# Duo attention into a gated FFT convolution: one hand-ordered list of 988 operations, in a new sequence and with 115 of them on another engine

## The chip, the core and the metric

The kernel runs on one core of a Trainium2 chip. The core's engines work side by side, each through its own list of instructions: TensorE (PE) for matmuls, VectorE (DVE), ScalarE (ACT) and GpSimd (POOL) for everything elementwise, and SyncE (SP), which here only issues DMA transfers. The metric is device microseconds for one execution. Three runs of the kernel before took 185.37, 185.87 and 186.39 us, so its time is the median, 185.87 us.

## The reference

Inputs are q, k and v of shape (4 batches, 8 heads, 768 positions, 64), a weight `w_proj` (512 x 1536), a filter (768 x 512) and a weight `w_out` (512 x 512), all float32. Four heads attend causally to everything ("retrieval", kind R), the other four only to 4 sink positions and a window of 64 (kind L). The attention's output is then gated and convolved along the sequence:

```python
scores = scale * np.matmul(q, k.transpose(0, 1, 3, 2))
scores = np.where(mask, scores, -1e9)            # causal, or sinks and window
a = np.exp(scores - scores.max(-1)); a = a / (a.sum(-1) + 1e-9)
x = np.matmul(a, v)                              # then heads side by side: (4, 768, 512)
x1, x2, x3 = np.split(x @ w_proj, 3, axis=-1)
y = x1 * np.fft.irfft(np.fft.rfft(x2, axis=1) * np.fft.rfft(filter_fft, axis=0), axis=1) * x3
return y @ w_out
```

(The quoted code is shortened; `is_retrieval` is the per-head vector that chooses the mask, and the reference's shapes are as told above.)

## The kernel before

**Units of work.** Attention goes by head pairs `n` = 0 to 15: batch `n // 4`, and within it the pairs in an order that gives the kinds RR, LL, RL, LL (6, 3, 5 and 3 chunks of scores). The convolution goes by batch. Its Fourier transforms are matmuls with tables `G` and `Gi` built at the start; the transform is split into folds so that it takes fewer products.

**The names.** Every step of the program is an operation with a short name, and each operation is one or a few instructions. For a pair n:

- `lk`, `lq`, `lv`: loads from DRAM on SP's queue (L876, L898). Pairs 0 and 1 have their q and k loaded before the list begins.
- `ck`, `cq` (or `cqk` for n of 8 and more), `cv`: casts to bf16 (through the helper `ev`, L533 to L541). `vx`, `vs`, `ks`: small copies of the rows for windows and sinks; `kz` sets their buffers to zero beforehand.
- `T`: transposes of q and k. For n below 8 on PE (L923), with `E` as eviction from PSUM; for n of 8 and more by DMA on SP's queue (L933).
- `sc`: score matmuls (L961), which use 64 rows of PE; `sb`: matmuls that add the mask for n below 4 (L972); `ex`: exponential on ACT (L978); `mk`: masks by multiplication on DVE for n of 4 and more (L988 to L1008).
- `at`: probabilities times v, with a column of ones that gives the sums (L1021); `rec` and `nm`: reciprocal and quotient on DVE (L1027, L1038).
- `tn`, `te`: transposes of the result and their eviction (L1094; some by DMA at L1103), which make `xT`, the left side of the projections.
- `fd`, `fe`, `fA`, `fS`, `fb`, `fr`: sums and differences of the folds (mostly through the helper `two`, L543); `W` (L1074 to L1082) and its eviction `We`.

For a batch b: `X` (L1125), spectrum of x2, and its eviction `Xe`; `pa`, `pb`, `pc`: products with the filter's spectrum, with `sw` as swaps of halves by DMA (L1150); `c`: inverse transform (L1190); `ce` its eviction; `x1` and `x3`: projections (L1160), `xs` eviction of one; `cv` with a batch, third and half (`cv0.1.0`): product of the convolution with the projection (L1201); `g` and `y`: gating products (L1179, L1183, L544); `o`: output projection (L1220, L1225); `oe`: eviction; `st`: store (L1243 to L1265). For the filter: `lfilt` (L739, issued on POOL's queue), `fold0`, `fold1` (L760, L756), `F` (L768), `H` (L775, L777). `lw` and `lwo` load the weights, also on POOL's queue (L747, L752). `chk` and `gd0` to `gd4` work out on DVE and PE whether the head flags and the sums allow this fixed program, and the program closes with the reading of a word (L1277).

**What sets the order.** A string `FAST` holds the names in one sequence, written out. The program walks through it once, and every instruction goes to its engine's list in that order:

```python
for word in FAST.split():
    name, _, slot = word.partition("@")
    name, _, eng = name.partition("/")
    now.update(slot=slot, engine=eng)
    ops[name]()
```

`@0` to `@3` names one of four PSUM slots of two banks each, which an operation may use when the last reader of the tile before it in that slot is done. `/v`, `/p`, `/s` and `/d` place a word on DVE, POOL, ACT or SP's DMA queue; words without a letter have a fixed engine. Each engine works strictly in its order: an instruction that waits holds up all that stand behind it on that engine. The same holds for the two queues that issue transfers, SP's and POOL's. Data dependences and slot reuse are turned into semaphores by the framework.

Of the kernel before, what the change touches and what calls it, by code (L numbers as in the profile page):

```python
# [1361 lines left out]
```

## Time and profile before

| | |
|---|---|
| median of 3 runs | 185.87 us (185.37 to 186.39) |
| profiled execution, span | 186.0 us |
| mean granted PE clock | 0.993 of full |
| PE busy | 171.6 us, 92% |
| DVE busy | 152.5 us, 82% |
| ACT busy | 142.2 us, 76% |
| POOL busy | 83.5 us, 45% |
| moved by DMA | 33.44 MB, 180 GB/s on average |
| chain that ended last | PE 65%, DMA 16%, ACT 4%, DVE 4% |

A line `L961 PE MATMUL f_sc<-f_qkT 64*128 64x128 bf16 x252 | 13.7, 218 | 0.7 <-DMA ...` reads: line 961 of the kernel, engine, operation, tile written and tile read, shape, how many; then their busy time in us and the mean ns of one; then how long the engine sat idle just before them and what ended that. In the table by stage each row is a stretch of the execution, followed by its length, then the busy time of each engine with its count of instructions, the granted clock, the busy share of DMA and the rate. In the list of waits a row is the waiting instruction, what released it, the total in us, how often, and the longest. In the chain that ended last a row is a start time, a length and what ran. Times are in us from the first instruction.

### The profile page before, as it was taken

The page shows a single profiled execution, that of the slowest core. Times are in us where ns is not written, and L with a number is a line of the kernel's source. Part 1 is how long each engine was busy: PE and PEld are TensorE (multiplying, and loading weights), DVE is VectorE, ACT ScalarE, POOL GpSimd, SP SyncE. Part 2 cuts the span into 40 slices and gives each one's busy share as a digit, 9 for nine tenths or more (in the row PEclk, how much of TensorE's full clock was granted, in tenths as well). Part 3 has the DMA queues.
Part 4 walks back from the last instruction along what each step waited for, and adds up shares of the span by engine and source line. Part 5 has one row for each costly group of instructions (what it writes and reads, how often), then busy time and mean ns, then how long its engine had stood idle before and what let it go on. Part 6 is the DMA issues. An engine that isn't in the chain of part 4 may idle for free.

```text
span 186.0 us, 4370 instructions
## 1 busy us (share of the span) xinstructions
PE 171.6 (92%) x1685; PEld 102.2 (55%) x1702; DVE 152.5 (82%) x297; ACT 142.2 (76%) x186; POOL 83.5 (45%) x99
## 2 busy tenths in 40 slices
...
GB/s 163 305 305 194 257 272 244 260 215 130 211 224 217 104 217 222 177 149 221 216 239 201 223 203 171 127 252 222 124 102 40 118 0 131 40 4 113 188 281 108
DMA packets 76836, 33.44 MB, mean 180 GB/s; under 512 B 66058, under 2 KB 73226, under 8 KB 76810
## 3 DMA queue, kind: packets, MB, share of 16 engines
...
q10 hardware_dynamic: 146, 0.13, 0.2%
q14 instruction: 12, 0.10, 0.1%
HBM read 24.64 MB, written 6.29 MB: 166 GB/s over the span
## 4 chain that ended last, share of the span: by engine, by line
PE 65%; DMA 16%; ACT 4%; DVE 4%; SPq 3%; POOL 3%; issue 2%; POOLq 0%
PE f_x_ps L1160 20%; PE f_out_ps L1225 10%; PE f_X_ps L1125 10%; DMA f_filt<-in_moe_filter_fft_dram 7%; PE f_c_ps L1190 7%; PE f_sc L961 6%; PE f_att L1021 4%; DMA f_qkT<-f_qk_bf 4%; DMA f_v_f<-in_v_dram 3%; SPq L898 3%; DMA qk_ahead<-in_q_dram 2%; PE f_xt_ps L1094 2%; PE f_F_ps L768 1%; POOL f_fo L544 1%; PE f_W_ps L1082 1%
## 5 line engine op out<-in xcount | busy, mean ns | idle before, releaser
L978 ACT ACTIVATE f_pT<-f_sc 128x1024 bf16<-128x1024 f32 (+2 forms) x68 | 58.3, 914 | 4.1 <-PE f_sc L972 2.1
L1160 PE MATMUL f_x_ps<-f_xT,f_wproj 128*128 128x384 bf16 x256 | 48.4, 326 | 0.1
L1160 PEld LDWEIGHTS <-f_wproj 128*128 128x128 bf16 x256 | 23.5, 98 | 15.6 <-issue 0.4
L961 PE MATMUL f_sc<-f_qkT 64*128 64x128 bf16 (+3 forms) x328 | 21.1, 242 | 2.2 <-ACT f_pT L978 0.8
L1125 PE MATMUL f_X_ps<-f_wproj,f_xh 128*128 128x512 bf16 x91 | 22.1, 379 | 0.3
L1225 PE MATMUL f_out_ps<-f_wout,f_gy 128*128 128x512 bf16 x85 | 22.0, 379 | 0.3
L544 POOL TENSOR_TENSOR f_gy<-turns,f_gy 128x768 bf16<-128x768 bf16 x7 | 11.6, 1669 | 20.8 <-DVE f_gy L1179 11.3
L1190 PE MATMUL f_c_ps<-f_Gi,f_P 128*128 128x384 bf16 x96 | 18.7, 326 | 0.1
L1021 PEld LDWEIGHTS <-f_pT 128*128 128x128 bf16 x472 | 16.4, 97 | 4.0 <-issue 1.5
L541 ACT COPY f_o<-f_out_ps 128x1024 f32<-128x1024 f32 (+2 forms) x15 | 11.5, 788 | 8.8 <-PE f_out_ps L1225 8.8
L961 PEld LDWEIGHTS <-f_qkT 64*128 64x128 bf16 x328 | 11.1, 94 | 12.6 <-issue 8.4
L1201 DVE TENSOR_TENSOR turns<-angle,f_c_ps 128x384 bf16<-128x384 f32 x32 | 16.4, 547 | 1.7 <-ACT angle L541 1.3
L1021 PE MATMUL f_att<-f_v_aug,f_pT 128*128 128x65 bf16 x392 | 17.3, 193 | 0.4 <-DVE f_attn L1038 0.4
L544 POOL TENSOR_TENSOR f_fo<-f_attn 128x384 bf16<-128x384 bf16 x11 | 10.9, 1003 | 14.6 <-PE f_W_ps L1082 12.2
L1038 DVE TENSOR_TENSOR f_attn<-f_att,f_recs 128x768 bf16<-128x768 f32 x16 | 15.3, 954 | 0.4
L541 ACT CAST f_X<-f_X_ps 128x1024 bf16<-128x1024 f32 x11 | 11.1, 1016 | 5.9 <-PE f_X_ps L1125 5.9
L544 POOL TENSOR_TENSOR f_br<-f_fo,f_uv 128x256 bf16<-128x256 bf16 x9 | 6.9, 766 | 18.7 <-DVE f_uv L544 9.1
L1125 PEld LDWEIGHTS <-f_xh 128*128 128x128 bf16 x96 | 8.9, 98 | 10.5 <-issue 1.0
L537 POOL CAST f_qk_bf<-qk_ahead 128x768 bf16<-128x768 f32 (+1 forms) x10 | 11.4, 1149 | 4.4 <-DMA qk_ahead<-in_k_dram 4.3
L1225 PEld LDWEIGHTS <-f_gy 128*128 128x128 bf16 x92 | 8.5, 98 | 8.8 <-issue 0.4
L541 ACT CAST f_xh<-f_W_ps 128x768 bf16<-128x768 f32 x12 | 9.5, 801 | 4.6 <-PE f_W_ps L1078 4.6
L1190 PEld LDWEIGHTS <-f_P 128*128 128x128 bf16 x96 | 9.1, 98 | 6.0
...
## 6 DMA issues: line engine op xcount, KB each, us to landing
...
```

The costliest lines, as they stand in the source:

```text
L537: nc.gpsimd.tensor_copy(out=out, in_=in_)
L541: nc.scalar.copy(out=out, in_=in_)
L544: (nc.gpsimd if now["engine"] == "p" else nc.vector).tensor_tensor(out, a, b, op)
L961: nc.tensor.matmul(sc[:, bank, col:col + 128 * cnt], lhsT=keys, rhs=qkT(n)[rows, 0, 128 * i:128 * (i + cnt)], start=(col == 0 or not biase ...
L978: nc.scalar.activation(out=pT(n)[:, c, :, 0:w], in_=held[f"sc.{n}.{c}"][:, :, 0:w], func=AF.Exp, scale=SCALE)
L1021: nc.tensor.matmul(att[:, hh, 65 * i:65 * i + 65], lhsT=pT(n)[:, c, bank, col:col + 128], rhs=values, start=(z == 0), stop=(z == len(here) ...
L1038: nc.vector.tensor_mul(attn(n).rearrange("p i hh d -> p hh i d"), rows[:, :, :, 0:64], recs()[:, n][:, :, :, None].to_broadcast([128, 2, N ...
L1125: nc.tensor.matmul(ps[:, u, :], lhsT=xh(b)[:, cc, chain, 128 * part:128 * part + 128], rhs=wproj()[:, cc, DM:2 * DM], start=(cc == 0), sto ...
L1160: nc.tensor.matmul(ps[:, s, 0:HS], lhsT=wproj()[:, cc, part * DM + cb * 128:part * DM + (cb + 1) * 128], rhs=xT(b)[:, cc, s * HS:s * HS + HS],
L1190: nc.tensor.matmul(ps[:, r, 0:HS], lhsT=P(b)[:, t, u, ch], rhs=Gi()[:, tile_no], start=(m == 0), stop=(m == 2))
L1201: fn(conv[:, half * HS:half * HS + HS], held[f"evs.{b}.{cb}"], held[f"c_ps.{b}.{cb}"][:, 1, 0:HS])
L1225: nc.tensor.matmul(ps[:, i % 2, :], lhsT=gy(b)[:, cb, i * 128:(i + 1) * 128], rhs=wout()[:, cb, :], start=(cb == 0), stop=(cb == NC - 1))
```

## The change

Only the string `FAST` changes. The set of 988 names is the same, and no operation's content or shape differs. What differs:

- the sequence of the words, and with it each engine's order, the order of the loads on SP's queue and of those on POOL's queue, and the PSUM slots;
- the engine of 115 casts, copies, sums and products: DVE to POOL 32, POOL to DVE 29, DVE to ACT 22, ACT to DVE 21, ACT to POOL 8, POOL to ACT 3.

The sequence was drawn up with a picture of the loads in which those under way at the same time share the DMA engines packet by packet.

The diff, cut to its beginning (up to the filter's `H` steps and the first `X`), the stretch from `W4` to the products of pair 6, the stretches around `T15` and `fb10`, and its end:

```diff
--- before.py
+++ after.py
@@ -61,66 +61,65 @@
 FAST = """
-angle2 angle1 turns1 turns2 wrap0 ones1 wrap2 blank2@0 ck0/p T0.1@2 wrap1 cq0/s blank0@1 ck1/p sin1 T0.0 size
-blank1@3 lk3 E0.0/v E0.1/v cos2 mtab3 T1.1@0 sin2 sc0.4@3 cos1 sc0.2@1 btab sb0.2 sc0.0@2 sb0.0 lq2 cq1/v cq2/p ex0.2
-T1.0 alt lq3 ex0.0 sc0.1@1 sb0.1 sb0.4 Gt0@2 E1.0/v E1.1/v sc0.3@0 ex0.4 sb0.3 ex0.1 sc1.1@3 lk2 Ge0/v sb1.1 sc0.5@2
-ex0.3 sc1.0@1 kz0/v cq3/p ex1.1 sb0.5 lv0 lv1 ck3/v ks1/p ck2/v lv2 cv0/p T2.0@0 sb1.0 ones0 ones2 T2.1 ex0.5 sc1.2@2
-T3.1@3 ex1.0 E2.0/v E2.1/v E3.1/s sb1.2 at0.1@1 ex1.2 at0.0 rec0 kz1/v T3.0 sc2.0@0 sc2.4@2 Gh0 nm0/v E3.0/s cv1/p
-kz2/p lv3 lfilt lk5 vx1/v sb2.0 ex2.4 sc3.1@3 Gt1@2 cv3/p ex2.0 vs1/v at1.1@1 lq5 Ge1/s sb3.1 sc2.1@0 ks2/p Gk1 sb2.1
-ex3.1 at1.0 ex2.1 tn0@2 cv2/s ck5/p Gh1 rec1 lk4 sc2.3@3 Gk0 sc3.0@0 te0/v sc2.2@2 lq4 nm1/v lk6 sb2.2 sb3.0 ex2.3
-fd0/v T5.1@1 fe0/v W0.0@3 lw1.0 vx3/v cq5/p vs2/v ck4/p vx2/v W0.1 ks3/v ex2.2 E5.1/s vs3/v ex3.0 at2.0@2 T5.0 We0/v
-E5.0/s at2.1 sc3.2@3 tn1@0 rec2 nm2/v lk7 te1/v sb3.2 tn2@1 fd1/v ex3.2 sc5.1@2 cq4/s te2/v fold1 lq6 fold0 T4.1@0
-at3.1@3 ex5.1 lv4 at3.0 fe2/v T4.0 F2.1@1 E4.0/s lw1.1 F2.0 fe1/v F0.1@2 fd2/v F0.0 rec3 E4.1/s nm3/v mk5.1 H0.0/v
-W1.0@0 H2.1/s W1.1 H2.0/s H2.2/s W2.1@3 W2.0 fd3/p H0.1/v sc5.0@1 We1/s sc4.2@0 ck6/p ex5.0 lw0.0 H0.2/v W3.0@2 ks5/p
-fe3/v We2/v cq6/p ex4.2 W3.1 We3/v sc4.0@1 sc4.1@3 ex4.0 ex4.1 F1.0@0 F1.1 sc4.3@2 sc4.4@1 X0.2.1@3 ck7/p H1.1/v
...
-lk10 cv0.1.0 cv0.1.1 vs6/s W5.0@1 vx6/s W5.1 at6.0@3 ce0.0/s vx7/s at6.1 y0.1/p g0.2 c0.3.1@2 c0.3.0 We5/s cv0.0.1
-ce0.3/s cv0.0.0 sc8.4@0 sc8.1@1 rec6 ex8.4 nm6/v lq10 lv8 ex8.1 W4.0@3 cqk9/p y0.0/v W4.1 We4/s c0.2.1@0 c0.2.0
...
-fA10/v W9.0@0 x12.0.0@3 ex12.1 ce1.1/s W9.1 fr10 vx13/s cv1.1.0 x12.0.1 mk12.0 c1.0.0@2 We9/s fb10/p cv12/p c1.0.1
-cv1.1.1 fA11/p xs2.0/v c1.3.1@0 W10.0@1 W10.1 fS11/p ce1.0/s fb11/p fr11 x32.0.1@3 x32.0.0 c1.3.0 We10/s vs13/s
...
-T15 at12.0@1 sc14.1@2 sc13.2@0 ex13.2 at12.1 rec12 X2.2.1 pb2.1/p nm12/v x12.2.1@0 x12.2.0 ex14.1 tn12 pb2.0/v
-sc14.4@2 sc14.0@1 Xe2.2/s xs2.2/s mk13.2 fe12/v ex14.4 fd12/v st0.3 o1.1.0@3 mk13.1 sc15.0@0 sc15.1@2 pc2.0/v ex14.0
...
-y3.3/v o2.3.1 o2.2.1 gd3@3 gd4 x33.3.0@0 x33.3.1 g3.3 o3.0.0@2 o3.1.0@3 o3.1.1 oe2.3/s oe3.1/s o3.0.1 o3.5.0@1 st2.3
-oe3.5/s o3.2.0@0 oe3.0/s o3.2.1 o3.3.0@3 oe3.2/s o3.3.1 st3.1/v st3.5/v o3.4.0@1 oe3.3/s o3.4.1 oe3.4/s st3.0/v
-st3.2/v st3.3/v st3.4/v o3.5.1@2 oe3.6/s st3.6/s
+angle2 wrap0 turns1 turns2 angle1 wrap1 ck0/p blank2@1 wrap2 cq0/s lk3 T0.1@3 size mtab3 lv0 lk2 ck1/p sin2 lq2 T0.0
+kz0/v E0.0/v blank0@2 blank1@0 E0.1/v sc0.5@3 sin1 cos1 btab cq1/p ones0 sc0.0@2 lq3 sc0.4@1 sb0.5 cos2 sb0.4 T1.0@0
+ck3/p sb0.0 lq4 E1.0/v T1.1 E1.1/v lv1 ex0.4 ex0.5 sc0.2@1 sc0.3@0 sb0.2 sb0.3 ex0.0 alt sc1.0@2 sb1.0 ex0.3 ex1.0
+ck2/p kz1/v sc1.1@0 Gh0 sb1.1 cv1/p ex0.2 ex1.1 cv0/v lfilt lv2 ones1 sc0.1@2 Gt0@3 cq2/v sb0.1 Gt1@1 vs1/p T2.0@0
+ex0.1 T2.1 Ge1/v E2.0/s E2.1/s at0.0@1 Ge0/v ks1/v cq3/v at0.1 T3.1@2 E3.1/s rec0 nm0/v sc2.3@0 ex2.3 T3.0 sc2.0@3
+lw1.0 sc2.1@1 sb2.1 ex2.1 E3.0/v sb2.0 sc1.2@0 fd0/p fe0/v cv2/v ex2.0 lv3 tn0@2 lk4 sb1.2 ex1.2 sc3.0@1 Gk1 lk5
+sc3.1@3 te0/v vx1/p lq5 ones2 sb3.0 ks2/v cv3/v cq4/p sb3.1 ex3.0 lw1.1 ex3.1 at1.1@0 sc2.2@2 ck4/v lw0.0 ks3/v sb2.2
+at1.0 ck5/s rec1 nm1/v sc2.4@1 W0.0@3 vx2/v W0.1 ex2.4 ex2.2 T4.1@0 vx3/v kz2/p lv4 We0/v E4.1/s fd1/p vs2/v cq5/p
+fe1/v T4.0 tn1@1 sc3.2@2 at2.0@3 lv5 at2.1 E4.0/s lq6 T5.1@0 E5.1/s vs3/v T5.0 sb3.2 te1/v rec2 ex3.2 W1.0@1 W1.1
+We1/s sc4.2@2 ex4.2 nm2/v Gh1 E5.0/v at3.0@3 sc5.0@0 fd2/p sc5.1@1 lq7 at3.1 ex5.0 fold1 F2.1@2 lk7 ex5.1 fold0 F2.0
+rec3 cv5/p nm3/v F0.1@0 fe3/v H2.1/s W2.0@1 W3.1@3 fd3/v cq6/p H2.0/s H2.2/v fe2/v W3.0 We3/v H0.2/s F0.0 W2.1 We2/v
+sc4.0@2 F1.1@3 H0.1/s cv4/v H0.0/s F1.0 ex4.0 sc4.5@0 sc4.1@1 X0.2.1@2 Hd1 Hd0 mk5.1 X0.2.0 H1.1/s lk6 H1.2/v ex4.1
...
+c0.3.1@3 T8 mr6 c0.3.0 fr5 ex6.3 lwo cv0.0.1 mk6.1 mk6.0 W5.0@2 W5.1 cv0.0.0 at6.0@1 vs6/s at6.1 y0.1/v rec6 We5/s
+vx7/s ce0.3/s nm6/v y0.0/p W4.0@0 lk10 sc8.4@2 W4.1 cv0.3.1 exp0 ex8.4 fe6/p We4/s cv0.3.0 c0.2.0@1 c0.2.1 sc8.2@3
...
+pc1.1/v pc1.0/v c1.1.0@1 ce1.1/s c1.1.1 g1.1 W9.0@2 fe11/v c1.0.1@0 fA10/v mk12.1 fS10/p fd11/p fr10 W9.1 cv1.1.0
+We9/v cv1.1.1 cqk13/s lk15 x12.0.1@3 c1.0.0 fS11/p x12.0.0 fb10/p fA11/p ce1.0/s xs2.0/s mk12.0 fr11 W10.1@2 W10.0
...
+X2.0.0 T15 mk12.2 X2.1.0 vs13/p x31.3.1@3 Xe2.0/s sc13.1@0 cv1.3.0 y1.3/v sc13.0@2 Xe2.1/v ex13.1 x31.3.0 g1.3
+at12.1@1 ks13/s at12.0 ex13.0 sc13.2@2 lv15 sc14.1@3 lv14 rec12 nm12/v ex13.2 ex14.1 mk13.1 X2.2.0@0 mk14.1 X2.2.1
+Xe2.2/s mk13.2 pb2.1/v pa2.0/p pb2.0/p mk13.0 x12.2.1@1 sc14.4@3 fd12/v ex14.4 pa2.2/v x12.2.0 st0.3 o1.1.0@0 sc14.0@3
+sw2.0 fe12/v vx13/p cv15/p fA12/v sc15.0@2 xs2.2/s ex14.0 sc15.1@1 ks15/v ex15.0 ks14/s mk15.0 pc2.0/v o1.0.0 o1.1.1
...
+cv3.3.0 o2.2.0 o2.2.1 oe2.5/s cv3.3.1 oe2.3/s x33.3.1@0 gd2 y3.2/v x33.3.0 y3.3/v o3.4.0@1 o3.0.0@3 g3.3 o3.5.0@2
+st2.5 o3.4.1 oe3.5/s o3.0.1 o3.1.0@0 oe3.4/s o3.1.1 o3.2.0@2 oe3.0/s oe3.1/s o3.5.1@1 oe3.6/v st2.3 st3.5/v o3.2.1
+o3.3.0@0 o3.3.1 st3.6/s st3.4/v st3.0/v oe3.2/v oe3.3/s gd3@0 gd4 st3.1/v st3.2/v st3.3/v
 """
```

More of the change, by code (lines that the diff above doesn't have):

```diff
@@ L99 @@
-lk14 sc12.1@2 ex12.3 fe11/p pc1.1/v lv14 sc12.0@0 fS10/v ex12.0 x31.1.0 c1.1.1@1 lq14 c1.1.0 g1.1 fd11/v mk12.2
-fA10/v W9.0@0 x12.0.0@3 ex12.1 ce1.1/s W9.1 fr10 vx13/s cv1.1.0 x12.0.1 mk12.0 c1.0.0@2 We9/s fb10/p cv12/p c1.0.1
-cv1.1.1 fA11/p xs2.0/v c1.3.1@0 W10.0@1 W10.1 fS11/p ce1.0/s fb11/p fr11 x32.0.1@3 x32.0.0 c1.3.0 We10/s vs13/s
-y1.1/p cv1.0.1 cqk13/s cv1.0.0 lq15 c1.2.0@1 y1.0/p W11.1@2 g2.0 lk15 W11.0 mk12.1 c1.2.1 ce1.3/v We11/s cqk14/s
-cqk15/p cv1.3.0 T13 X2.0.0@3 ce1.2/v T14 X2.1.1@2 cv1.3.1 X2.1.0 Xe2.1/s cv1.2.0 X2.0.1 x31.3.0@0 sc13.0@2 Xe2.0/s
@@ L104 @@
-cv1.2.1 sc13.1@1 y1.3/v ks13/s x31.3.1 cv14/p y1.2/v pa2.1/v lv15 g1.3 st0.5 ex13.1 ex13.0 pa2.0/p X2.2.0@3 mk13.0
-T15 at12.0@1 sc14.1@2 sc13.2@0 ex13.2 at12.1 rec12 X2.2.1 pb2.1/p nm12/v x12.2.1@0 x12.2.0 ex14.1 tn12 pb2.0/v
-sc14.4@2 sc14.0@1 Xe2.2/s xs2.2/s mk13.2 fe12/v ex14.4 fd12/v st0.3 o1.1.0@3 mk13.1 sc15.0@0 sc15.1@2 pc2.0/v ex14.0
-ex15.0 fS12/v cv15/v o1.0.0 ex15.1 at13.1@1 pa2.2/v ks15/s at13.0 o1.1.1 rec13 x32.2.1@0 fA12/v fb12/p nm13/v o1.0.1
-x32.2.0 o1.3.0@2 sc15.2@1 ks14/s oe1.1/s mk14.0 g2.2 pc2.1/v vx15/s ex15.2 sc14.3@3 ex14.3 sw2.0 sw2.1 sc14.2@0
```

69 lines of the change are left out of this document (36 added, 33 removed).

## The prediction

> **What bounds the kernel now.** I read the page first (busy shares, slices, the chain that ended last), then the table by stage, then what TensorE (PE) waited for, then the chain at the places where those waits lie.
>
> ```profile
> PE 171.6 (92%) x1685; PEld 102.2 (55%) x1702; DVE 152.5 (82%) x297; ACT 142.2 (76%) x186; POOL 83.5 (45%) x99
> PE 65%; DMA 16%; ACT 4%; DVE 4%; SPq 3%; POOL 3%; issue 2%; POOLq 0%
> ```
>
> ```profile
> core 0: us, PE busy (x) PEld busy (x) DVE busy (x) ACT busy (x) POOL busy (x), PEclk, DMA share, GB/s
> 0.00:6.00 6.00, 4.42 (x16) 1.60 (x17) 4.75 (x12) 3.37 (x6) 4.34 (x16) 1.00 0.61 201
> 6.00:12.00 6.00, 4.45 (x44) 2.19 (x42) 4.91 (x8) 5.97 (x8) 1.27 (x3) 1.00 0.94 311
> 12.00:18.00 6.00, 5.76 (x97) 4.01 (x96) 4.63 (x7) 5.98 (x9) 3.08 (x7) 1.00 0.96 215
> 18.00:24.00 6.00, 4.47 (x86) 3.34 (x84) 3.70 (x9) 4.35 (x7) 3.74 (x6) 1.00 0.92 266
> 24.00:30.00 6.00, 5.68 (x92) 4.21 (x91) 5.62 (x14) 5.53 (x7) 3.12 (x5) 1.00 1.14 244
> 30.00:36.00 6.00, 4.41 (x57) 2.60 (x56) 4.53 (x10) 3.91 (x6) 0.00 (x0) 1.00 1.17 268
> 54.00:72.00 18.00, 17.71 (x190) 11.06 (x187) 17.30 (x32) 16.53 (x23) 10.10 (x10) 1.00 1.10 189
> 72.00:102.00 30.00, 29.73 (x329) 17.38 (x332) 27.90 (x64) 28.90 (x38) 15.72 (x16) 1.00 1.07 202
> 102.00:130.00 28.00, 27.26 (x269) 16.67 (x269) 25.39 (x47) 24.12 (x31) 17.70 (x13) 1.00 0.98 199
> 150.00:180.00 30.00, 29.79 (x164) 16.05 (x166) 18.80 (x32) 12.04 (x17) 9.04 (x5) 1.00 0.28 99
> ```
>
> From 54 to 180 us PE is short of full by only 0.29 + 0.27 + 0.74 + 0.21 us in these four stages. So PE's own work sets the time there, although DVE (17.30 of 18) and ACT (28.90 of 30) have hardly more room. From 6 to 36 us PE lacks 1.55 + 0.24 + 1.53 + 0.32 + 1.59 = 5.2 us: only the opening has much to win. The waits say for what:
>
> ```profile
> PE f_F_ps L768 <- DVE f_fold L760: 1.4, 1, 1.4
> PE f_att L1021 <- DVE f_v_x L535: 0.9, 1, 0.9
> PE f_sc L961 <- DMA f_qkT<-f_qk_bf: 0.6, 1, 0.6
> PE f_W_ps L1082 <- DVE f_attn L1038: 0.3, 1, 0.3
> ```
>
> The largest is the filter's first product `F`. The chain leads from it back to a load:
>
> ```profile
> 18.75 0.83 POOL f_v_aug L537
> 19.98 13.21 DMA f_filt<-in_moe_filter_fft_dram
> 33.22 0.97 DVE f_fold L760
> 34.23 0.39 PE f_F_ps L768
> ```
>
> The filter is issued on POOL's queue behind the cast `cv1`, takes 13.21 us to land among the loads of SP's queue, is folded on DVE, and only then can `F` run.
>
> **The opening in the new order.** `lfilt` again stands behind `cv1/p`, and `cv1` needs the load `lv1`. In the new list one transfer more stands ahead of `lv1` on SP (`lq4`, beside k3, v0, k2, q2 and q3, which are ahead of it in both): 384 KB at the 311 GB/s of 6 to 12 us are 1.2 us; the 0.41 us of other POOL work between `cv1` and the issue goes. So the issue comes near 19.98 + 1.2 − 0.4 = 20.8, and with the same 13.2 us the filter lands at 34.0 and `F` starts at 35.0, 0.8 us later than 34.23. PE's words after `F2.1` are the same amount of work as before (143.5 us against 143.6, each word at its median spacing in the trace), so this would be 0.8 us on the end. Against it: further on the new list is ahead. `X0.2.1` has 136.7 us of PE work behind it where the old one had 134.8, that is, it was put 1.9 us of PE work earlier, and the casts and evictions in front of it, at their durations, let it start near 42 to 43.5. With the old start of 43.79 this gives a result between 0.1 earlier and 1.6 later.
>
> ```profile
> 43.79 2.70 PE f_X_ps L1125 x12
> ```
>
> The bounds: if the filter lands when it did and its fold keeps PE from waiting, the 1.4 us go; if both the load and the rest of my walk come late, +1.6. I take **+0.1**, the middle of these two: the walk stacks each cast behind the one before it on its engine and so errs to the late side.
>
> **Visits to the scores.** Score matmuls (`sc`) use 64-row tiles; all else is 128 rows. A visit costs more than its matmuls:
>
> ```profile
> 52.59 1.30 PE f_x_ps L1160 x8
> 54.56 0.63 PE f_sc L961 x14
> 55.19 1.41 PE f_x_ps L1160 x8
> 59.14 0.33 PE f_sc L961 x5
> ```
>
> Eight x products take 1.30 us, but 1.41 where scores follow: 0.11 on the way in. Fourteen score matmuls take 0.63 and five 0.33, so one takes 0.033 and 0.17 is left for the way out. I estimate 0.28 us a visit. Counting unbroken runs of `sc` among PE's words, the old list has 38 and the new one 43, one of the five ahead of `F`, where PE waits anyway. The other four fall where PE is full: 4 x 0.28 = **+1.1** (bounds 0, if each falls into a wait, and 5 x 0.28 = 1.4).
>
> **Waits that go.** The scores of pair 15 waited for their transposes by DMA:
>
> ```profile
> 122.45 6.53 DMA f_qkT<-f_qk_bf
> 129.03 0.56 PE f_sc L961 x14
> ```
>
> In the new list 9.0 us of PE work lie between the word of `T15` and `sc15.0`, before 5.3; the transfer of 6.53 fits, **−0.6**. The wait of `W` (0.3) is at 71 us, where `W4` takes PSUM slot 3, which pair 6's quotient `nm6` has to empty; in the new list `W4` takes slot 0, whose last readers, the products `cv0.0`, stand further ahead: **−0.3**, and 0 at the least.
>
> **Waits that come.** `fb10` now stands on POOL behind `fS10`, `fd11` and `fS11`, and `W10` wants it. By POOL's durations of such products (about 0.8 to 1.0 us each) `W10` comes 0 to 0.5 us late: **+0.2**.
>
> **The engines' loads.** The moves go both ways. The two-input products dominate:
>
> ```profile
> L544 DVE TENSOR_TENSOR f_fo<-f_attn 128x384 bf16<-128x384 bf16 x21 | 8.6, 423 | 0.0
> L544 POOL TENSOR_TENSOR f_fo<-f_attn 128x384 bf16<-128x384 bf16 x11 | 10.9, 1003 | 14.6 <-PE f_W_ps L1082 12.2 <-DVE f_attn L1038 2.2
> L541 ACT CAST f_v_aug<-f_v_f 128x768 bf16<-128x768 f32 x7 | 5.8, 835 | 0.0
> L537 POOL CAST f_v_aug<-f_v_f 128x768 bf16<-128x768 f32 x7 | 6.0, 855 | 2.9 <-DMA f_v_f<-in_v_dram 2.9
> ```
>
> Summed over all 115 with such rows (each op at its mean on the old and the new engine): DVE −4.1 us, ACT −3.7, POOL +5.7. The largest parts: five net casts `cv` leave ACT (5 x 0.835 = 4.2; three go to POOL, two to DVE), four net `fd` go from DVE to POOL (−1.7, +4.0), three net `fe` and two net `y` come the other way. The five copies `vx` that come to POOL (64 x 520) have no row there; they lie between 0.53 (the cast's 0.855 for 768, by length) and that cast's whole 0.855, so POOL may gain up to 1.6 us more, while it has over 50% idle. What does the relief earn? PE lacks 1.5 us in the four stages after 54 us, and the 0.6 and 0.3 above are most of it, so I cost the rest at **0** (bounds −0.6, and the rival of exclusion below). It is hidden by PE's own work; a DVE that slowed instead would have no cover between 54 and 72 us, 0.7 us free.
>
> **The tail.** The old list ends on a 256-wide output tile, the new one on `oe3.3`, 512 wide:
>
> ```profile
> 181.10 0.38 ACTq L1243 DMA_DIRECT2D out_dram<-f_o  x1
> L541 ACT COPY f_o<-f_out_ps 128x512 f32<-128x512 f32 x5 | 2.9, 586 | 2.6 <-PE f_out_ps L1225 2.6
> L541 ACT COPY f_o<-f_out_ps 128x256 f32<-128x256 f32 x2 | 0.8, 375 | 0.0
> ```
>
> 0.586 − 0.375 = **+0.2**. The store that follows it ends the span (186.0) 4.9 us after its issue at 181.10, and so it would again. `gd3` and `gd4`, moved behind `oe3.3`, are short and end under that store; without it they would add their own length.
>
> **Sum.** 186.0 (the span profiled) + 0.1 + 1.1 − 0.6 − 0.3 + 0.2 + 0.2 = 186.7. The median of the runs shown, 185.87, is 0.13 below the profiled span, so **186.6 us**: slightly slower, inside the 0.5% (184.94 to 186.80) that a measurement of this kernel can tell from no change. Its own range is 185.2 to 187.7.
>
> **Rivals.** *The opening gains.* If the filter lands at 33.2 again and the wait of 1.4 at `F` goes, the opening gives −1.4 in place of +0.1, and two of the four visits fall into waits that are left: 186.6 − 1.5 − 0.6 = **184.5**. For it: only there PE lacks time, and DMA is the one resource whose use was drawn up anew. Against it: the issue of the filter hangs on `lv1`, which has one load more ahead.
>
> *ACT stuck at `ck5` (slower).* `ck5/s` moves from POOL to ACT, into the middle of the evictions and exponentials ahead of `F`, and must wait for `lk5`. Walking ACT's new list with its durations, ACT arrives there near 26.4. SP's loads up to `lk5` are 15 of 384 KB, 5.8 MB; the rates above (201 GB/s before 6 us, then 311, 215, 266, 244) give 6.0 MB by 24 us and 7.4 by 30, from which the filter and weights take up to half after 20.8. So k5 lands near 26, between 24 and 28. From 26.4 on, each us late holds `E4`, `E5`, `We1` and the exponentials behind it, and so the H products and `X0`. At 28: 186.6 + 1.6 = **188.2**. Against it: PE's `F` waits for the filter till 35 anyway and covers some of it.
>
> *DVE and POOL exclude each other.* A mask of 128x768 shows it:
>
> ```profile
> 63.77 0.81 POOL L544 TENSOR_TENSOR f_br<-f_fo,f_uv 128x256 bf16<-128x256 bf16 x1
> 63.98 1.02 DVE L996 TENSOR_TENSOR f_pT<-f_pT,mtab 128x768 bf16<-128x768 bf16 x1
> 101.71 0.54 DVE L996 TENSOR_TENSOR f_pT<-f_pT,mtab 128x768 bf16<-128x768 bf16 x1
> ```
>
> Beside a POOL product it took 1.02 us, without one 0.54: 0.48 lost to a POOL instruction with 0.60 still to run. If each of the 5.7 us added on POOL costs DVE up to 0.48/0.60 = 0.8 of itself, DVE loses 4.6 where it was to win 4.1. Where DVE is at 96% (54 to 72 us) it then sets the pace; with two thirds of the 4.6 already covered by DVE's idle time (33 us in all), 1.0 to 1.5 us remain: 186.6 + 1.2 = **187.8**. Against it: the moves are spread, and POOL's additions lie partly where DVE has room (150 to 180 us, 18.8 of 30). The Trainium skill, "SBUF — State Buffer", section "Who interferes with whom", says that a DVE instruction with two inputs in SBUF contends with a GpSimd instruction that reads SBUF, and calls the shared port pair an exclusive lock; these rows agree.
>
> *It changes nothing.* Terms of both signs cancel, 185.9.
>
> **How the numbers follow.** Forecast 0.42, opening gains 0.24, ACT stuck 0.16, exclusion 0.10, nothing 0.08. Faster by over 0.5%: 0.24 x 0.8 + 0.42 x 0.1 + 0.08 x 0.2 = 0.25. Slower: 0.42 x 0.35 + 0.26 x 0.75 = 0.34. Same: the rest, 0.41. The range reaches to the gain and to the stuck ACT: 184.3 to 188.3.
>
> **What would show it.** Right: `F` starts at 34.5 to 35.5 with its wait on the fold about as long as now; no wait of pair 15's scores on DMA; PE busy up by about 1; the weight loads of scores show five more idle spells. Wrong, on the fast side: `F` at 34 or earlier with no wait. ACT stuck: an idle spell of ACT ahead of the cast of `ck5`, released by DMA. Exclusion: DVE's busy time not 4 us lower, its masks and `fA` longer than now. The prediction falls if `X0.2.1` starts before 41.5 or after 45, or if the new order shows a wait of PE of over 1 us after 54 us.

## The result, and the profile after

The changed kernel takes 205.34 us (median of four runs, 204.77 to 206.53), the kernel before beside it 186.13 us. The ratio is 1.103, with a 95% interval of 1.098 to 1.109: slower by a tenth, far outside the range of 184.3 to 188.3 us. Times here are medians of all runs of a kernel; ratios and their intervals leave out runs more than 1.5% above that kernel's fastest. A run's time lies some 1.5 us above its span (204.93 us with a span of 203.3), so spans are compared with spans below: 203.3 after, 186.0 before. They differ by 17.3 us where the medians differ by 19.2, since the execution of before that was profiled is one of its longer ones: of seven others on record six span 184.2 to 185.3 us.

The page after, busy shares and the chain that ended last (the after kernel's lines have numbers smaller by one, since the string is one line shorter):

```profile
PE 175.9 (87%) x1689; PEld 102.6 (50%) x1702; DVE 170.1 (84%) x293; ACT 139.2 (68%) x182; POOL 95.8 (47%) x107
PE 39%; DVE 30%; ACT 15%; DMA 5%; issue 4%; POOL 3%; SPq 1%; ACTq 0%; POOLq 0%; DVEq 0%
```

DVE's share of the chain went from 4% to 30%, and its busy time from 152.5 to 170.1 us. By the rows of before it should have done 4.1 us *less*. ACT is shorter by 3.0, as expected (3.7). POOL is longer by 12.3 where 5.7 were expected. The table by stage after:

```profile
54.00:72.00 18.00, 16.35 (x198) 10.84 (x196) 17.61 (x30) 12.27 (x17) 9.55 (x10) 1.00 0.77 137
72.00:102.00 30.00, 28.84 (x318) 16.91 (x317) 25.76 (x51) 25.26 (x34) 18.02 (x17) 1.00 1.04 198
102.00:130.00 28.00, 23.24 (x211) 13.95 (x212) 27.43 (x43) 20.57 (x27) 17.02 (x19) 1.00 0.80 144
```

Between 102 and 130 us PE now lacks 4.76 us (0.74 before), while DVE is busy 27.43 of 28. PE's waits after, the largest and the one at `F` (total in us, how often, the longest; a wait of 1.5 us in the opening, the same before, is left out):

```profile
PE f_sc L960 <- DVE f_qkT L534: 3.9, 3, 1.6
PE f_qkT_ps L922 <- ACT f_qkT L540: 3.0, 4, 0.9
PE f_c_ps L1189 <- ACT angle L540: 2.8, 3, 1.6
PE f_att L1020 <- DVE f_pT L995: 1.7, 1, 1.7
PE f_att L1020 <- DVE f_pT L1007: 1.3, 1, 1.3
PE f_qkT_ps L922 <- DVE f_qkT L534: 0.9, 1, 0.9
PE f_F_ps L767 <- ACT f_HAB L776: 0.6, 1, 0.6
```

None of the waits that the prediction dealt with is left (the filter's, the transposes of pair 15, `W4`), but new kinds have come. The loss splits as follows. The last output product ends 14.4 us later (195.0 against 180.6), and 2.9 us come behind it; together they are the 17.3 us of span. The 14.4 can be divided by an estimate: if each word of PE's list is given its usual length and the sum is taken off its start time, what remains is the time PE has lost so far, and by the last output products it was 14.2 us before and 27.5 after. So some 13.3 us are waits of PE in the course of the kernel, and some 1.2 are PE's own work (the five visits to the scores, at the price taken in that sum, 0.24 us each).

**First kind: DVE is held up by POOL.** Groups of DVE instructions, before and then after (busy us, mean ns of one):

```profile
L1201 DVE TENSOR_TENSOR turns<-angle,f_c_ps 128x384 bf16<-128x384 f32 x32 | 16.4, 547 | 1.7 <-ACT angle L541 1.3 <-PE f_c_ps L1190 0.2
L1038 DVE TENSOR_TENSOR f_attn<-f_att,f_recs 128x768 bf16<-128x768 f32 x16 | 15.3, 954 | 0.4
L996 DVE TENSOR_TENSOR f_pT<-f_pT,mtab 128x1024 bf16<-128x1024 bf16 x12 | 8.5, 711 | 0.1
L544 DVE TENSOR_TENSOR f_P<-f_P,f_m 128x1024 bf16<-128x1024 bf16 x10 | 6.7, 681 | 0.0
L535 DVE CAST f_qk_bf<-qk_ahead 128x768 bf16<-128x768 f32 x3 | 1.6, 530 | 0.0
```

```profile
L1200 DVE TENSOR_TENSOR turns<-angle,f_c_ps 128x384 bf16<-128x384 f32 x32 | 16.6, 546 | 2.1 <-ACT angle L540 1.2 <-PE f_c_ps L1189 0.9
L1037 DVE TENSOR_TENSOR f_attn<-f_att,f_recs 128x768 bf16<-128x768 f32 x16 | 15.3, 957 | 0.6
L995 DVE TENSOR_TENSOR f_pT<-f_pT,mtab 128x1024 bf16<-128x1024 bf16 x12 | 13.3, 1110 | 0.0
L543 DVE TENSOR_TENSOR f_P<-f_P,f_m 128x1024 bf16<-128x1024 bf16 x10 | 9.7, 982 | 0.1
L534 DVE CAST f_qk_bf<-qk_ahead 128x768 bf16<-128x768 f32 x5 | 4.8, 950 | 0.0
```

The same twelve masks take 1110 ns on the mean in place of 711, ten products of the same shape 982 in place of 681, casts from float32 950 in place of 530. These means mix undisturbed instructions with a few very long ones: before, eleven of the twelve masks took 0.67 to 0.69 us and one 1.07; after, six took 0.62 to 0.68 and six 0.84 to 2.50. Of the five casts after, one took 2.48 us and the others 0.55 to 0.60. Instructions that read one of their operands from PSUM did not change: 547 and 546 ns for the sums and differences at L1201 (`cv0.1.0` and the like, which join the two halves of the inverse transform), 954 and 957 for the quotients `nm`. POOL pays as well: its casts of v take 991 ns where they took 855. The timeline shows what a single case looks like:

```profile
111.89 2.23 POOL L543 TENSOR_TENSOR f_P<-f_P,f_m 128x1024 bf16<-128x1024 bf16 x1 [3.76 <-DVE f_m L543]
112.17 2.50 DVE L995 TENSOR_TENSOR f_pT<-f_pT,mtab 128x1024 bf16<-128x1024 bf16 x1
114.72 0.20 PE L1020 MATMUL f_att<-f_v_x,f_pT 128*128 128x65 bf16 x1 [1.69 <-DVE f_pT L995]
```

POOL's product `pc1.2` starts at 111.89 and ends at 114.12; the mask that starts beside it at 112.17 ends at 114.67, 0.55 us after POOL, about as long as such a mask takes alone. PE waits 1.69 us for it.

**Second kind: an eviction between the halves of a tile.** A PSUM tile of two banks is filled in two halves by two words (`T4.1` and `T4.0`). Timeline after, around pair 4's transposes:

```profile
28.33 0.51 PE L922 MATMUL f_qkT_ps<-identity,f_qk_bf 128*128 128x128 bf16 x6
28.88 0.80 ACT L540 COPY f_qkT<-f_qkT_ps 128x768 bf16<-128x768 bf16 x1
29.73 0.44 PE L922 MATMUL f_qkT_ps<-identity,f_qk_bf 128*128 128x128 bf16 x5 [0.89 <-ACT f_qkT L540]
```

In the new list `E4.1`, the eviction of the first half, stands ahead of `T4.0`. The second six transposes then wait 0.89 us for it, although they write the other bank. The lines for `f_qkT_ps` (3.0 and 0.9), `f_c_ps` (2.8) and `f_F_ps` (0.6) above are all of this kind: 7.3 us. What releases PE is a semaphore of the program that follows the eviction. Whether the framework sets it for the tile as a whole, or the banks themselves would need it, no run here separates.

**Third: behind the last output product** 8.3 us pass to the end of the span (195.0 to 203.3), where 5.4 passed before (180.6 to 186.0). The last row of the timeline after is the word that all engines read before they close:

```profile
195.95 0.20 DVE L660 TENSOR_SCALAR other<-f_rows_right,differ 1x1 int32<-1x1 f32 x1 [0.94 <-PE f_rows_right L655]
```

It is written at 196.16, and the end comes 7.1 us later. Before, the same word was written at 174.8, 11 us ahead of the end. POOL's closing then ran from its reading of the word (174.81) to the end of a long drain at 179.98, beside PE's last products; after, it runs from 196.19 to 202.45, behind everything else. The last store landed at 184.9 before, 1.1 us ahead of the end, and at 197.7 after, 5.6 us ahead.

### The profile page after: what moved, and what is told of

Its sections match the earlier page's. It is cut to its first block, busy times and chain, and to the rows that moved or that the text cites. A ratio compares the mean times of both kernels' runs of the same rounds, so it can differ in the third digit from the quotient of the medians.

```text
span 203.3 us, 4387 instructions
## 1 busy us (share of the span) xinstructions
PE 175.9 (87%) x1689; PEld 102.6 (50%) x1702; DVE 170.1 (84%) x293; ACT 139.2 (68%) x182; POOL 95.8 (47%) x107
## 4 chain that ended last, share of the span: by engine, by line
PE 39%; DVE 30%; ACT 15%; DMA 5%; issue 4%; POOL 3%; SPq 1%; ACTq 0%; POOLq 0%; DVEq 0%
PE f_x_ps L1159 9%; ACT f_pT L977 6%; PE f_out_ps L1224 6%; PE f_c_ps L1189 5%; DVE f_pT L995 5%; PE f_att L1020 4%; PE f_sc L960 3%; DMA f_v_f<-in_v_dram 3%; PE f_X_ps L1124 3%; DVE f_qkT L534 3%; DVE turns L1200 2%; PE f_qkT_ps L922 2%; ACT f_qkT L540 2%; PE f_sc L971 2%; DMA qk_ahead<-in_k_dram 2%
## 5 line engine op out<-in xcount | busy, mean ns | idle before, releaser
L977 ACT ACTIVATE f_pT<-f_sc 128x1024 bf16<-128x1024 f32 (+3 forms) x68 | 59.1, 915 | 15.7 <-PE f_sc L960 11.4
L1159 PE MATMUL f_x_ps<-f_xT,f_wproj 128*128 128x384 bf16 x256 | 47.8, 327 | 0.0
L960 PE MATMUL f_sc<-f_qkT 64*128 64x128 bf16 (+3 forms) x328 | 22.2, 242 | 4.7 <-DVE f_qkT L534 3.9
L1224 PE MATMUL f_out_ps<-f_wout,f_gy 128*128 128x512 bf16 x88 | 23.0, 380 | 0.3
L1189 PE MATMUL f_c_ps<-f_Gi,f_P 128*128 128x384 bf16 x96 | 19.2, 326 | 2.8 <-ACT angle L540 2.8
L960 PEld LDWEIGHTS <-f_qkT 64*128 64x128 bf16 x328 | 11.4, 94 | 17.5 <-issue 11.7
L543 POOL TENSOR_TENSOR f_uv<-f_fo 128x256 bf16<-128x256 bf16 x12 | 9.9, 827 | 18.2 <-DVE f_fo L543 11.1
L543 POOL TENSOR_TENSOR f_m<-f_X,f_HAB 128x1024 bf16<-128x1024 bf16 x4 | 8.5, 2118 | 19.7 <-ACT f_X L540 19.7
L995 DVE TENSOR_TENSOR f_pT<-f_pT,mtab 128x1024 bf16<-128x1024 bf16 (+1 forms) x18 | 17.5, 971 | 0.0
L543 POOL TENSOR_TENSOR f_fo<-f_attn 128x384 bf16<-128x384 bf16 x12 | 13.0, 1085 | 9.3 <-DVE f_attn L1037 5.7
L536 POOL CAST f_v_aug<-f_v_f 128x768 bf16<-128x768 f32 x10 | 9.9, 991 | 7.3 <-DMA f_v_f<-in_v_dram 7.2
```

The lines of the kernel that those rows point to most:

```text
L543: (nc.gpsimd if now["engine"] == "p" else nc.vector).tensor_tensor(out, a, b, op)
L960: nc.tensor.matmul(sc[:, bank, col:col + 128 * cnt], lhsT=keys, rhs=qkT(n)[rows, 0, 128 * i:128 * (i + cnt)], start=(col == 0 or not biase ...
L977: nc.scalar.activation(out=pT(n)[:, c, :, 0:w], in_=held[f"sc.{n}.{c}"][:, :, 0:w], func=AF.Exp, scale=SCALE)
L995: nc.vector.tensor_mul(some, some, tab.to_broadcast([128, 2, cols, 128]))
L1159: nc.tensor.matmul(ps[:, s, 0:HS], lhsT=wproj()[:, cc, part * DM + cb * 128:part * DM + (cb + 1) * 128], rhs=xT(b)[:, cc, s * HS:s * HS + HS],
L1189: nc.tensor.matmul(ps[:, r, 0:HS], lhsT=P(b)[:, t, u, ch], rhs=Gi()[:, tile_no], start=(m == 0), stop=(m == 2))
```

## Experiments

The theories: *halves* (the order of words within a tile), *exclusion* (DVE held up by POOL), *tail* (the last word). Each was undone in the changed kernel, and put alone into the kernel before.

### Halves undone

```diff
 (nine words, each moved behind the second half of its tile)
-E4.1/s fd1/p vs2/v cq5/p fe1/v T4.0          -c1.1.0@1 ce1.1/s c1.1.1
+fd1/p vs2/v cq5/p fe1/v T4.0 E4.1/s          +c1.1.0@1 c1.1.1 ce1.1/s
 (likewise E1.0, E3.1, E5.1, E7.1, ce0.0, ce2.0, H0.2)
```

> The changed kernel with nine words moved: an eviction or scaling that stands between the two halves of one PSUM tile (E1.0, E3.1, E4.1, E5.1, E7.1, ce0.0, ce1.1, ce2.0, H0.2) goes behind the second half. Theory of the halves: the second half's matmuls wait for the first half's eviction although it reads the other bank; the waits of transposes for ACT (3.0 us) and DVE (0.9), of the inverse transform for ACT (2.8) and of F for ACT (0.6) go, 7.3 us in all, and the time falls by 5 to 7 us, to about 199. Rival, that DVE sets the pace because POOL holds it up: those waits go, but PE then waits for DVE's masks and evictions instead, and the time falls by 0 to 2 us.

Measured: 200.93 us, ratio to before 1.074 (1.065 to 1.083), 4.4 us less than the changed kernel. The waits of transposes, inverse transform and `F` are gone from the list. The largest that are left all name DVE:

```profile
PE f_sc L960 <- DVE f_qkT L534: 3.9, 4, 1.8
PE f_att L1020 <- DVE f_pT L995: 1.7, 1, 1.7
PE f_att L1020 <- DVE f_pT L1007: 1.3, 1, 1.3
PE f_W_ps L1081 <- DVE f_fo L543: 1.1, 1, 1.1
```

The fall lies between the two expectations: the waits go as the theory of the halves says, but only 4.4 of their 7.3 us are earned, and the rest is waited for elsewhere.

### Tail undone

```diff
-... gd1 ...                  -... gd2 ... oe3.3/s gd3@0 gd4
+... gd1 gd2 ...              +... x33.3.1@0 gd3@1 gd4 ...
```

> The changed kernel with gd2, gd3 and gd4 moved from behind the last eviction to about 187 us (gd2 behind gd1, gd3 and gd4 behind x33.3.1). Theory of the tail: the last word gd4 writes is read by every engine before it closes, and POOL's closing takes 6 us after that (its drain begins 3.7 us after its last branch), so the time falls by 2.5 to 3.5 us. Rival, that the span ends with the last store as before: it falls by 0.5 at most.

Measured: 202.11 us, ratio 1.084 (1.074 to 1.094), 3.2 us less (its runs are 200.35, 201.27, 202.96 and 207.01, so the size is uncertain by a microsecond or more). In the profile 5.5 us lie between last output product and end, where there were 8.3.

### Engines and sequence crossed

```diff
 (sequence after, the 115 letters of before)     (sequence before, the 115 letters of after)
-cv0/v ... fd0/p ... y0.0/p                      -cv0/p ... fd0/v ... y0.0/v
+cv0/p ... fd0/v ... y0.0/v                      +cv0/v ... fd0/p ... y0.0/p
```

> The changed kernel's sequence, with the 115 operations on the engines that they had before. If the moves to other engines are the cause (POOL 5.7 us more work, DVE's two-input products run into it): DVE's busy time falls back toward 152 to 158 us and the time to 193 to 197, with the waits for halves and the tail left. If the sequence is the cause: DVE's busy time stays over 163 and the time over 200.

> The sequence of before, with the 115 operations on their new engines. If the engines are the cause: DVE's busy time rises to 163 or more and the time to 193 to 198. If the sequence is: 186 to 190.

Measured: 229.70 us (ratio 1.228, 1.219 to 1.238) and 220.59 us (1.182, 1.174 to 1.190). Both are far slower than either kernel, with single waits of PE of up to 3.7 us. By the letter the first result fits its second branch (DVE busy 163.5 us, over 163, and a time over 200), which speaks for the sequence; the second fits neither branch (DVE 172.6 us, but 220.6 in place of 193 to 198). At these sizes the pair doesn't tell engines from sequence: the two were drawn up together, and with foreign letters an engine stands at words which its list reaches too early or too late. It shows only how much each order rests on its letters: 24 us in the one case, 34 in the other.

### Both undone together

```diff
-T4.1@0 ... E4.1/s ... T4.0   (and the other eight)   -oe3.3/s gd3@0 gd4
+T4.1@0 ... T4.0 E4.1/s                               +x33.3.1@0 gd3@1 gd4
```

> The changed kernel with the nine words moved behind the second halves and with gd2 to gd4 moved forward, both edits together. The two alone gave 200.93 and 202.11 us where the changed kernel had 205.34. If they are independent: 205.3 - 4.4 - 3.2 = 197.7 us, and some 11 us over before remain for DVE and POOL. If the waits only move from one place to another: over 199.

Measured: 200.79 us (ratio 1.075, 1.066 to 1.084), no better than the halves alone. The tail did shrink (5.5 us), but the last output product ends 2.6 us later than with the halves alone (194.0 against 191.4). By the sum over PE's words it was 0.9 us ahead at 45 us and 2.8 behind by 60. The two timelines show what lies between, first the kernel with the halves undone, then the one with both:

```profile
52.04 3.19 POOL L543 TENSOR_TENSOR f_m<-f_X,f_HAB 128x1024 bf16<-128x1024 bf16 x1 [10.37 <-ACT f_X L540]
52.09 0.56 DVE L534 CAST f_qk_bf<-qk_ahead 128x768 bf16<-128x768 f32 x1
```

```profile
51.15 2.13 POOL L543 TENSOR_TENSOR f_m<-f_X,f_HAB 128x1024 bf16<-128x1024 bf16 x1 [10.16 <-ACT f_X L540]
51.20 2.49 DVE L534 CAST f_qk_bf<-qk_ahead 128x768 bf16<-128x768 f32 x1
```

In both POOL's `pb0.1` and DVE's cast `ck6` start 0.05 us apart. In the first the cast takes its usual 0.56 and POOL's product is stretched from 2.13 to 3.19; in the second POOL goes first and the cast takes 2.49. The two programs have the same words up to 180 us, and POOL's recorded start is the earlier one by the same 0.05 us in both, so these records don't show what decides. One such meeting is worth 1.9 us to DVE. These are the profiles of one execution each; that the same outcome repeats in the timed runs is likely from their medians, and not shown.

### POOL writes without reading

On top of both edits:

```diff
-(nc.gpsimd if now["engine"] == "p" else nc.vector).tensor_tensor(out, a, b, op)
+if now["engine"] == "p":
+    nc.gpsimd.tensor_tensor(out[few], a[few], b[few], op)   # 8 columns
+    nc.gpsimd.memset(out, 0.5)
+    nc.gpsimd.memset(out, 0.5)
+else:
+    nc.vector.tensor_tensor(out, a, b, op)
```

> The kernel with both edits, in which POOL's sums and products (fd, fe, fA, fS, fb, pa, pb, pc, y) leave out their work: each computes 8 columns of its last dimension, which keeps what it waits for, and then fills its output twice with a constant, a write without a read, to last about as long as before (0.9 to 2.1 us). Theory of exclusion (a DVE instruction that reads two operands from SBUF, or copies fp32 there, waits until POOL's reading instruction ends): DVE's masks and products return to their short durations (128x1024 masks from 1.11 to about 0.7 us), DVE's busy time falls by 8 to 13 us (what is left belongs to POOL's casts, which still read), and the time falls by 4 to 8 us below the kernel with both edits. Rival, that DVE's long instructions are covered or that any POOL activity does it: DVE's durations and the time stay within 1.5 us.

Measured: 194.19 us, 6.6 less than with both edits. Its four runs are 191.76, 192.74, 195.63 and 195.96; the lower two (192.25 between them) lie 8.4 us below the median of the three runs with both edits that count in the ratio above (200.61). The page and the groups of masks, products and casts, first of the kernel with both edits:

```profile
PE 176.2 (88%) x1689; PEld 102.8 (52%) x1702; DVE 170.0 (85%) x293; ACT 139.4 (70%) x182; POOL 95.2 (48%) x107
```

```profile
L995 DVE TENSOR_TENSOR f_pT<-f_pT,mtab 128x1024 bf16<-128x1024 bf16 x12 | 13.8, 1154 | 0.0
L543 DVE TENSOR_TENSOR f_P<-f_P,f_m 128x1024 bf16<-128x1024 bf16 x10 | 9.8, 983 | 0.1
L534 DVE CAST f_qk_bf<-qk_ahead 128x768 bf16<-128x768 f32 x5 | 4.7, 939 | 0.0
```

Then with POOL's writes in place of its sums and products:

```profile
PE 175.7 (92%) x1689; PEld 102.8 (54%) x1702; DVE 152.9 (80%) x293; ACT 139.1 (73%) x182; POOL 98.8 (52%) x201
```

```profile
L1001 DVE TENSOR_TENSOR f_pT<-f_pT,mtab 128x1024 bf16<-128x1024 bf16 x12 | 9.9, 823 | 0.0
L549 DVE TENSOR_TENSOR f_P<-f_P,f_m 128x1024 bf16<-128x1024 bf16 x10 | 7.0, 708 | 0.4 <-POOL f_P L547 0.3
L534 DVE CAST f_qk_bf<-qk_ahead 128x768 bf16<-128x768 f32 x5 | 2.8, 560 | 0.0
```

POOL is busy as long as before the edit (98.8 us against 95.2), and DVE has the same instructions, yet DVE's busy time falls by 17.1 us (170.0 to 152.9), more than the 8 to 13 expected: masks from 1154 to 823 ns, products from 983 to 708, casts from 939 to 560. Which masks stayed long tells the cause. Two of them, the first beside a fill by POOL that was under way, the second beside a cast by POOL:

```profile
130.51 0.95 POOL L547 MEMSET f_m<- 128x1024 bf16 x1
130.97 0.68 DVE L1001 TENSOR_TENSOR f_pT<-f_pT,mtab 128x1024 bf16<-128x1024 bf16 x1
132.21 1.17 POOL L536 CAST f_v_aug<-f_v_f 128x768 bf16<-128x768 f32 x1
132.61 1.30 DVE L1001 TENSOR_TENSOR f_pT<-f_pT,mtab 128x1024 bf16<-128x1024 bf16 x1
```

Masks of this size that run beside fills take 0.68 to 0.69 us, and the three long ones (1.10, 1.30, 1.38) each start beside a copy or cast of POOL, which still reads. For DVE's instructions with two operands in SBUF it is POOL's *reading* that holds them up. The Trainium skill, "SBUF — State Buffer", section "Who interferes with whom", says the same: a DVE instruction with two inputs in SBUF contends with a GpSimd instruction that reads SBUF, and not with one that only writes. These runs agree with both halves of the sentence, and the unchanged 547 and 954 ns of the instructions that read PSUM agree with its statement on DVE instructions with at most one SBUF input, which leaves out those in modes that use both of DVE's ports.

For copies and casts within SBUF the reading is not the condition. A fill by POOL holds them up too, as in the changed kernel:

```profile
26.07 0.84 POOL L850 MEMSET f_v_x<- 64x520 bf16 x1
26.37 0.57 DVE L534 COPY f_qkT<-f_qkT 128x16 bf16<-128x16 bf16 x1
```

Copies of this shape take 0.16 to 0.17 us alone, and the fill some 0.5. With both edits a cast of v took 0.93 beside such a fill, 0.55 alone. That the five casts from float32 above are short in this experiment doesn't show the opposite: none of them starts behind a fill.

### Four products to DVE

```diff
-pb0.1/p ... pc1.2/p ... pb3.1/p ... pa3.1/p
+pb0.1/v ... pc1.2/v ... pb3.1/v ... pa3.1/v
```

> The kernel with both edits and four products of 128x1024 (pb0.1, pc1.2, pb3.1, pa3.1) back from POOL to DVE. On POOL they hold up six DVE instructions by 2.0 + 0.7 + 2.0 + 0.9 + 1.8 = 7.4 us in the profile of the changed kernel. Theory of exclusion: DVE pays 4 x 0.7 = 2.8 us more and saves 7.4, its busy time falls by 4 to 5 us although it does more, and the time falls by 1.5 to 4 us. Rival, that POOL's relief of DVE is worth what it was moved for: DVE's busy time rises by 2 to 3 us, and the time is the same or up to 2 us longer.

Measured: 197.31 us (ratio 1.059, 1.052 to 1.066), 3.5 us less than with both edits. Three of the four are moves of the change; `pb3.1` stands on POOL in the kernel before as well. DVE's busy time went down by 4.5 us though it has four instructions more, as the theory of exclusion has it:

```profile
PE 175.7 (89%) x1689; PEld 102.7 (52%) x1702; DVE 165.5 (84%) x297; ACT 139.3 (71%) x182; POOL 85.5 (43%) x103
```

### Three products to POOL, in the kernel before

```diff
-pb0.1/v ... pc1.2/v ... pa3.1/v
+pb0.1/p ... pc1.2/p ... pa3.1/p
```

> The kernel before with three of the change's moves alone: the products pb0.1, pc1.2 and pa3.1 (128x1024) go from DVE to POOL. DVE loses 3 x 0.7 = 2.1 us of work, POOL gains 3 x 2.1 to 2.35 = 6.6. Theory of exclusion: DVE's instructions that start beside these three are held up to their ends, by 1 to 2 us each as in the changed kernel; DVE's busy time rises by 1 to 4 us although it has less to do, and the time rises by 1 to 4 us. Rival, relief: DVE's busy time falls by about 2 us and the time is within 1 us.

Measured: 192.85 us, ratio 1.028 (1.019 to 1.037): slower by 5.8 us, more than the 1 to 4 expected. DVE's busy time rose from 152.5 to 157.3 us with three instructions less. The timeline and PE's largest wait:

```profile
100.74 2.17 POOL L543 TENSOR_TENSOR f_P<-f_P,f_m 128x1024 bf16<-128x1024 bf16 x1 [1.29 <-DVE f_m L543]
100.84 2.61 DVE L995 TENSOR_TENSOR f_pT<-f_pT,mtab 128x1024 bf16<-128x1024 bf16 x1
```

```profile
PE f_att L1020 <- DVE f_pT L995: 3.0, 1, 3.0
```

Three of the 115 moves, alone in the order of before, cost 2.8%. A relief of DVE by 2.1 us became a load of 4.8.

### Evictions between halves, in the kernel before

```diff
-c0.0.0@0 c0.0.1 ... ce0.0/s          -T7.1@2 T7.0 ... E7.1/s
+c0.0.0@0 ce0.0/s c0.0.1              +T7.1@2 E7.1/s T7.0
 (likewise ce1.0, ce3.0, E6.1)
```

> The kernel before with one pattern of the change alone: five evictions (ce0.0, ce1.0, ce3.0, E6.1, E7.1) stand between the two halves of their PSUM tile, not behind both. Theory of the halves: the second half waits for the eviction each time, about 0.5 us for ce and 0.9 for E, and PE gets new waits for ACT at the inverse transform and the transposes of 3 x 0.5 + 2 x 0.9 = 3.3 us; the time rises by 1.5 to 3.5 us. Rival, that the halves are free of each other and the waits in the changed kernel came from elsewhere: no such waits, and the time within 0.7 us.

Measured: 190.94 us, ratio 1.023 (1.015 to 1.031): slower by some 4 us, and the waits are there in the places where the words were put, 4.1 us where 3.3 were expected:

```profile
PE f_c_ps L1189 <- ACT angle L540: 2.3, 3, 1.2
PE f_qkT_ps L922 <- ACT f_qkT L540: 1.8, 2, 0.9
```

### The last word last, in the kernel before

```diff
-... gd3@3 gd4 x33.3.0@0 ... oe3.6/s st3.6/s
+... x33.3.0@0 ... oe3.6/s gd3@0 gd4 st3.6/s
```

> The kernel before with gd3 and gd4 moved behind the last eviction oe3.6, where the changed kernel has them. Theory of the tail: all engines read the last word only then, POOL's closing steps no longer run ahead, and the time rises by 2.5 to 3.5 us. Rival: the last store covers it, under 0.7 us.

Measured: ratio 1.002 (0.998 to 1.006), no difference. The theory's size falls here. In its profile, which is of its longest run (189.25 us), 7.2 us pass behind the last output product, 1.8 more than before. The word is written 0.3 us behind that product here (1.1 in the changed kernel, where `gd3` waits 0.72 us for `oe3.3`), and the closing takes 6.9 us from there, while the last store lands 2.6 us behind the product, not 4.3. So the late word costs what the closing is longer than the stores, at most 2 us in this kernel by one profile, and the timed runs don't show even that. Why the undoing in the changed kernel earned 3.2 us and this cost nothing is not settled.

### The filter's load ahead of `cv1`, in the kernel before

```diff
-cv0/p ... cv1/p kz2/p lv3 lfilt
+cv0/p lfilt ... cv1/p kz2/p lv3
```

> The kernel before with one word moved: lfilt stands directly behind cv0 and so ahead of cv1 on POOL's queue, not behind it. The filter's load is issued some 4 us earlier (before 19.98, in the changed kernel 18.94 with landing at 29.8). If the wait of F for the filter (1.4 us) was a delay of the end: it goes, and the time falls by 0.5 to 1.4 us. Rival, that the loads of k and v which share the DMA engines come later by what the filter takes: the wait moves to another place, and the time is within 0.5 us.

Measured: 190.55 us, ratio 1.023 (1.017 to 1.029): slower. `F` doesn't wait for the filter any more, but v3's load lands at 26.2 where it landed by 21.2. Its cast then holds POOL's list, and behind it the copy `ks2`, for which PE waits 3.2 us (the row of POOL's timeline, and PE's wait):

```profile
26.45 0.83 POOL L536 CAST f_v_aug<-f_v_f 128x768 bf16<-128x768 f32 x1 [7.49 <-DMA f_v_f<-in_v_dram]
```

```profile
PE f_sc L960 <- POOL f_qkT L536: 3.2, 1, 3.2
```

The rival of this run has the mechanism right, and its size wrong: 4.3 us in place of 0.5 at the most.

### Two small moves in the opening, in the kernel before

```diff
-cv1/p kz2/p lv3 lfilt lk5 ... vs1/v
+cv1/p lv3 lfilt vs1/p kz2/p lk5 ...
```

> The kernel before with two small moves on POOL in the opening: kz2 goes behind the filter's load, and the copy vs1 goes from DVE to POOL ahead of cv3, which held it up by 0.7 us on DVE and with it the products at1 (wait of 0.9 us). The load of v1 keeps its place, unlike where the filter was put ahead of cv1 (190.55 us). If the two waits (0.9 us and part of F's 1.4) are on the path: the time falls by 0.3 to 0.9 us. If F's wait for the filter takes up what is won: within 0.3 us. If the copy on POOL delays cv3 and what follows: slower by up to 1 us.

Measured: ratio 1.002 (0.997 to 1.008), no difference. The waits for `f_v_x` and for the filter are gone, and others have come in (2.7 us of transposes waiting for POOL's casts). Nothing tried here beats the kernel before.

## Why the prediction was wrong

The predicted 186.6 us left out one mechanism (the halves), took a second for covered (the tail), and had the third, the largest, as a rival with small chance and size (the exclusion). Its own signs of being wrong came: `X0.2.1` started after 45, PE has waits of 1.3 to 1.7 us after 54 us, and DVE's masks are longer with its busy time up, not down by 4.

- **"I cost the rest at 0" (the engines' loads).** This is the step that failed most. Each moved operation was priced at its mean on the new engine, as if the engines were free of each other. The rival of exclusion was the right mechanism, with the right row (1.02 against 0.54 us), but with a chance of 0.10 and 1.2 us. Measured: DVE's busy time is 17.1 us longer with POOL's sums and products reading than with fills in their place, and the end comes 6.6 us later (8.4 by the lower runs). The rival's estimate took the rate from one short POOL instruction (0.48 us lost) and let a third of the loss through. The loss isn't a rate: it is the remaining length of the POOL instruction that came first, up to 1.9 us beside products of 2.1 to 2.2 us (the cast of 2.49 us that takes 0.56 alone). The order of before kept these meetings rare. The 18 masks of L996 (L995 after) overlapped POOL's work for 3.5 us before and 11.3 after, by adding up the overlaps in both traces. I had read the longer masks in the old trace and didn't ask how often the new list would produce them.
- **The halves** were not in the prediction at all. 7.3 us of waits, 4.4 us of the end. They could be read from the diff, since `E4.1/s` stands ahead of `T4.0` there, and from the old list, where evictions mostly stand behind both halves. In the old list `E3.1/s` and `E5.1/s` stood ahead of `T3.0` and `T5.0` too, with products (`at0`, `at2.0`) between, which hid it. I priced the new list's PE words as if only the slot mattered.
- **The tail**: "+0.2", with `gd3` and `gd4` that "end under that store". The span behind the last output product grew by 2.9 us. What I took for covered is followed by the closing of every engine, 7.1 us from the word to the end. That the span would again end with the last store fails too: the store landed 1.1 us ahead of the end before and 5.6 us ahead of it after. Undoing the late word earned 3.2 us, but the same word put late into the kernel before cost nothing, so the tail's share of the time is the least certain of the three.
- **The opening**: "the filter lands at 34.0 and `F` starts at 35.0". The filter was issued at 18.94 and landed 10.9 us later, at 29.8, 3.4 us earlier than before. The load `v1` came earlier (18.05, before 18.63), not later, though one more load was ahead of it: its second half was issued at 11.32 in place of 12.70. But `F` started at 36.95 all the same: PE's words ahead of it waited for evictions between halves (0.9, 0.9) and the fold stood on DVE behind `E5.0` and ran at 34.71, though its data had been there since 29.8. What DMA gained was never used. `X0.2.1` began at 45.10, outside my bounds of 42 to 43.5 and 1.3 us later than before. Its place in the list is also less far ahead than I took it: behind it the new list has `sc4.3`, `sc4.4` and `tn2` more and `sc4.5` fewer, which is 0.7 us at the usual spacing of these words, not 1.9. So the term of +0.1 was some 2 us too small, and the waits between halves are part of that.
- **The visits**: the five more are there, and the part of the idle time ahead of the scores' weight loads that the profile puts down to "issue" went from 8.4 to 11.7 us (the pages' rows for these loads). Their price was not measured by itself. **Waits that go**: right, pair 15's scores and `W4` wait no longer. They were worth 0.9 us, against 13 of new ones. **Waits that come**: `W10` (+0.2) doesn't wait; it follows the product ahead of it at once.
- **ACT stuck at `ck5`**: wrong. k5 landed at 23.8, ahead of ACT.

What is left: with both edits and with fills in place of POOL's sums and products, the profile (of the run of 192.74 us) spans 191.3 us, 5.3 more than before. By the sum over PE's words, 1.2 are put down to the visits and 3.7 to waits of PE (17.9 against 14.2), 2.2 of them by 55 us, in whose course the first scores wait for `E0` and `E1` on DVE; 0.3 lie behind the last output product (5.7 against 5.4). In times the kernel is 8 us over before by the median of its four runs, and 6 by the lower two. That is not split by cause: POOL's casts and copies still read, and the parts undone one by one don't add up (the halves 4.4, the tail 3.2, both together 4.6).
